# Two row tiles of each of the first two experts closed with the sixth chunk of tokens

## The chip, the cores and the metric

The kernel runs on one core of a Trainium2 chip. The metric is the device time of one execution in microseconds (us), as a median of runs. The engines are TensorE (PE in the profile; its weight loads are PEld), VectorE (DVE), ScalarE (ACT), GpSimd (POOL) and SyncE (SP), which issues most of the DMA transfers.

## What is computed

Three layers follow one another on 2304 tokens: attention over 32 memory slots (`q`, `k`, `v`, `phi`; 4 batches of 576 tokens), a gated layer of width 1536 (`moe_w_gate`, `moe_w_val`, `moe_w_out`), and a mixture of eight experts with two experts chosen for each token. The change touches the last layer alone. Its input `x` is the output of the gated layer, 2304 x 512:

```python
logits = x @ w_gate
noise_scale = np.log1p(np.exp(x @ w_noise))
noisy_logits = logits + noise_scale * noise
top2 = np.argpartition(-noisy_logits, 2, axis=1)[:, :2]
...
for e in range(E):                       # E = 8 experts, F = 1024
    for k in range(2):
        mask = top2[:, k] == e
        h = np.maximum(x[mask] @ w1[e], 0.0)
        out[mask] += top2_w[mask, k, None] * (h @ w2[e])
```

## The kernel before

**Tokens.** The gated layer is done in two stages. `stage1` (line 412) makes the gated activations `gT`, `stage2` (435) multiplies them by `w_out` for one tile of 128 tokens at a time (18 tiles), into a PSUM tile `px`. Two tiles are a chunk, nine chunks in all (0 to 8). When a tile's `px` is complete, `tokens` (446) scales it and splits it into two float16 halves (`row`, on ScalarE and VectorE), writes it to the table `xs` in HBM, and has it transposed by a DMA into `xt`; then TensorE computes its router logits (`pl`, twelve small products, line 472), and once a chunk's two tiles are there `route` (526) finds the two best experts of each token. It counts the rows of each expert with small products on TensorE (`pk`, lines 570 to 573, which need the VectorE tile `o` of line 565), and GpSimd scatters each token's number and weight into the table `meta` at the slot that the count gives (four indirect DMAs per chunk, line 588).

**Experts.** Each expert has 624 slots, as five row tiles of 128, 128, 128, 128 and 112. For a row tile the kernel reads its token numbers from `meta` (`fetch`, 735, tile `mts`), gathers the rows from `xs` by GpSimd (`gather`, 749, tile `xg`, four buffers), and has SyncE transpose them (`turn`, 756) into the columns of `xe`, which has two buffers, one per expert. `first2` (759) multiplies `xe` by `w1` in eight steps `f`, each of 12 matmuls per span of columns, and ScalarE and VectorE turn the result `ph` into the hidden tile `hT` (770 to 772). `second2` (774) multiplies `hT` by `w2`, 24 matmuls of 512 columns per row tile, into `py`; ScalarE scales it into `y` (785) and GpSimd adds it to the output in HBM by a scatter (786). `moe2` (809) runs over the eight experts.

**Rows before the last token.** So that TensorE has work while the last tokens are routed, a part of the rows is closed early: after chunk `SNAP` the count of an expert is raised, if it is lower, to the number of early slots (lines 595 to 603), so that those slots are settled. Before, three tiles of expert 0 (`EARLY = 3`) are closed with the seventh chunk (`SNAP = 6`): `early_rows` (794) gathers and transposes them, the first product of 384 columns runs in `build` (1055), then the late rows are fetched, and the second products of the three tiles run (1066) while expert 0's last two tiles are gathered. `moe2` then does the other 240 columns of expert 0, its two last tiles, and the other experts with two spans of 312 columns.

**Weights.** Experts 0 and 1 have their weights split into float16 halves beforehand; they are loaded by line 733 into `w1a`, `w2a`, `w1b`, `w2b`. From expert 2 on `splits` (683) does it beside the products: each quarter of a weight is loaded into one of seven buffers (`wo`, line 675), squared and summed (701, 703), the sum goes through a small product on TensorE (`pmx`, line 86), and the quarter is split into `w1a`, `w2a`, `w1b` or `w2b` (378, 379) when the expert that used that buffer is through.

**Order.** Each engine runs its queue in order. A scheduler places the instructions by the order and the priorities of the program; the `yield`s of `tokens` and `route` (`WAIT_TURN`, `WAIT_ROUTE`, and their shorter `..._LAST` forms from chunk `SNAP` on) say how many steps later TensorE's part follows.

Of the kernel before, what the change touches and what calls it, by code (L numbers as in the profile page):

```python
# [10 lines left out]
F32 = mybir.dt.float32  # L11
# [5 lines left out]
ALU = mybir.AluOpType  # L17
# [8 lines left out]
E, F2 = 8, 1024  # L26
P = 128
# [3 lines left out]
F2T = F2 // P  # L31
CH = 256
# [7 lines left out]
ST = 5  # L40

TAIL = 112
SLOT = (ST - 1) * P + TAIL
PADS = ST * P

EARLY = 3
SNAP = 6

AHEAD2 = 2

# [15 lines left out]
class Kern:  # L66
# [379 lines left out]
    def tokens(self, c, t):  # L446
# [18 lines left out]
        nc.sync.dma_start_transpose(xt, row.rearrange("p a b -> p (a b)"))  # L465
        for _ in range(WAIT_TURN if c < SNAP else WAIT_TURN_LAST):
            yield
# [58 lines left out]
    def route(self, c, lg, it):  # L526
        nc, rp = self.nc, self.rp
# [27 lines left out]
        mt = rp.tile([P, nt, 2, 2], I32, tag="mt", name="mt")  # L555
# [9 lines left out]
        nc.vector.tensor_tensor(o, oh[:, :, 0, :], oh[:, :, 1, :], op=ALU.add)  # L565
        for _ in range(WAIT_ROUTE if c < SNAP else WAIT_ROUTE_LAST):
            yield
        pk = self.pr.tile([P, 512], F32, tag="pr", name="pk")[:, : nt * E].rearrange("p (t e) -> p t e", t=nt)
# [17 lines left out]
        for t in range(nt):  # L586
            for k in range(2):
# [6 lines left out]
                self.scatters.append(d)  # L594
        if c == SNAP:

            pk = self.pr.tile([P, 512], F32, tag="pr", name="pk")
            nc.tensor.matmul(pk[:1, :1], self.ones[:, :1], self.oacc[:, :1], start=True, stop=True)
            fr = rp.tile([1, 1], F32, tag="fr", name="fr")
            nc.vector.tensor_scalar(fr, pk[:1, :1], -1.0, float(EARLY * P), op0=ALU.mult, op1=ALU.add)  # L600
            nc.vector.tensor_scalar(fr, fr, 0.0, None, op0=ALU.max)
            nc.vector.tensor_tensor(self.oacc[:1, :1], self.oacc[:1, :1], fr, op=ALU.add)
            self.snapped = True


# [186 lines left out]
        others.append(d)  # L792

    def early_rows(self):
        xg = [self.gather(self.mt[(0, i)], PADS + (SNAP + 1) * CH) for i in range(EARLY)]
        yield
        yield
        for i in range(EARLY):
            yield
            self.turn(xg[i], self.xe[0], i)  # L800

    def xe_tile(self, e):
        self.xe[e] = self.mx.tile([P, 2 * KT, ST * P], F16, tag="xe", name="xe")
# [5 lines left out]
    def moe2(self):  # L809

        self.freed, self.nparts = [0, 0], 0
        self.splitter = self.splits()
        mt, xe, xg = self.mt, self.xe, {}
        for e in range(E):
            nx = e + 1
            if nx < E:
                self.xe_tile(nx)
                if e:
                    self.fetch(nx, 0, ST, self.scatters)
                for i in range(4):  # L820
                    xg[i] = self.gather(mt[(nx, i)])
            spans = [(0, SLOT // 2), (SLOT // 2, SLOT)] if e else [(EARLY * P, SLOT)]
            for f in range(F2T):
                self.first2(self.w1[e % 2], xe[e], f, spans)
                self.step2(2)
            self.freed[0] = e + 1
            todo = list(range(0 if e else EARLY, ST))
            sums = [] if e else self.sums0
            turns = list(range(ST)) if nx < E else []
            for n, i in enumerate(todo):  # L830
                self.second2(self.w2[e % 2], self.iw[:, e : e + 1], mt[(e, i)], i, sums, P if i < ST - 1 else TAIL)
                for _ in range(-(-len(turns) // (len(todo) - n))):
                    j = turns.pop(0)
                    self.turn(xg[j], xe[nx], j)
                    if j == 0:
                        xg[4] = self.gather(mt[(nx, 4)])
                self.step2(3)
            self.freed[1] = e + 1
# [61 lines left out]
    def build(self):  # L900
        tc, nc, ctx = self.tc, self.nc, self.ctx
# [27 lines left out]
        side, offset = [], {}  # L929

        def ahead_by(n):
            return tc.high_priority(n) if n else ExitStack()

        def step(n=1):
            for _ in range(n):
                for g in list(side):
                    with ahead_by(offset.get(g, 0)):
                        done = next(g, self) is self
                    if done:
                        side.remove(g)  # L940
# [40 lines left out]
        def first(b, u, ch):  # L981
            while self.tokens_ready < b * S + (ch + 1) * QC:
                turns(atts)
            if (b, u) not in self.wq:
                self.fold(b, u)
            self.stage1(b, u, ch)
# [19 lines left out]
        def beside():  # L1006
            nonlocal pre
            step()
            turns(atts)
            if pre is None and self.attended == B:  # L1010
                for _ in atts:
                    pass
                self.att_ctx.close()
                self.presplit_open()
                pre = start(self.presplits())
            if self.snapped and not self.mt:
                self.fetch(0, 0, EARLY, self.scatters)
                rows.append(start(self.early_rows()))

        def second(*Ts):  # L1020
            for T in Ts:
                for fs in (range(0, 4), range(4, 8), range(8, 12)):
                    self.stage2(T, list(fs))
                    beside()
                g = start(self.tokens(*divmod(T, CH // P)))
                if T >= NT - CH // P:
                    offset[g] = AHEAD

        for b in range(1, B):
            second(*range(3 * (b - 1) // 2 * TB, 3 * b // 2 * TB))  # L1030
            if b == B - 1:
                while pre is None:
                    beside()
                drain(pre)
                self.ps_ctx.close()
                self.early_open()
                self.wload2(0, 0)
                for e in range(AHEAD2):
                    self.inverse_scale(e)
                self.xe_tile(0)  # L1040
            self.fold(b, 0)
            for u in range(UN):
                if u + 1 < UN:
                    self.fold(b, u + 1)
                for ch in range(S // QC):
                    first(b, u, ch)
                    beside()
            self.folded = b + 1
# [3 lines left out]
        second(*range(3 * (B - 1) // 2 * TB, NT))  # L1052
        while not rows or rows[0] in side:
            beside()
        for f in range(F2T):
            self.first2(self.w1[0], self.xe[0], f, [(0, EARLY * P)])
            beside()
        while side:
            step()
        self.fetch(0, EARLY, ST, self.scatters)  # L1060
        late = [self.gather(self.mt[(0, i)]) for i in range(EARLY, ST)]
        self.wload2(1, 0)
        self.wload2(1, 1)
        self.fetch(1, 0, ST, self.scatters)
        self.sums0 = []
        for i in range(EARLY):
            self.second2(self.w2[0], self.iw[:, 0:1], self.mt[(0, i)], i, self.sums0)
            if i >= EARLY - len(late):
                j = i + len(late)
                self.turn(late[j - EARLY], self.xe[0], j)  # L1070
        self.moe2()
        self.overflow()
        self.ring_ctx.close()
# [30 lines left out]
```

## Time and profile before

| | us |
|---|---|
| Median of three runs (905.08 to 908.67) | 905.18 |
| The profiled execution's own time | 898.48 |
| Its span, first to last instruction | 896.7 |
| PE busy in the span | 813.6 (91%) |
| VectorE, ScalarE, GpSimd busy | 470.7, 450.4, 207.5 |

TensorE is busy for nine tenths of the span, so the time is its work and its gaps. A row of a timeline gives the start, the length, the engine, the line, what is written from what, and in brackets how long the engine sat idle before it and what ended that. In the view by stretches PEclk is the share of full speed that TensorE's clock was granted: 1.00 is 2.4 GHz, 0.50 is 1.2 GHz. Times are us from the start of the span.

### The profile page before, as it was taken

Reading aid. Unit: us, or ns where it says so; the run is one execution under the profiler, and the core shown is the slowest. Engines: PE = TensorE matmul, PEld = TensorE weight load, DVE = VectorE, ACT = ScalarE, POOL = GpSimd, SP = SyncE. Lnnn points to the kernel's source line nnn. Section 1 sums busy time; section 2 is a strip of 40 time slices with the busy share of each in tenths; the row PEclk is TensorE's granted clock in tenths of the full one; section 3 lists DMA queues with packets and bytes.
Section 4 is the critical chain, followed back from the end, with each engine's and each line's share of the span. In section 5 each row is a group of like instructions: output and inputs, shape, how many; then the busy total and the mean of one; then the engine's idle time right before and its main releaser. Section 6 shows DMA issues by size and latency. Waiting matters only on the chain. (4 is left out here: it accounts for less than half of the span.)

```text
span 896.7 us, 16818 instructions
## 1 busy us (share of the span) xinstructions
PE 813.6 (91%) x6531; PEld 534.5 (60%) x6531; DVE 470.7 (52%) x1317; ACT 450.4 (50%) x909; POOL 207.5 (23%) x210
## 2 busy tenths in 40 slices
PE   5368789889999999999959999999999999999995
PEld 4247665579645775687425666564746556574752
DVE  1778786576446986875433245463544346340110
ACT  3578675455333873763114456464545446461320
POOL 1544440020002120120132530232323122232112
PEclk9998789999999999999979999999999999999998
DMA  9598739710263566605782993686566867473213
GB/s 310 161 287 255 220 122 353 208 54 2 68 195 75 190 205 172 212 2 154 223 201 59 208 226 106 140 190 162 116 181 132 167 140 205 78 112 49 27 14 45
DMA packets 125922, 135.15 MB, mean 151 GB/s; under 512 B 71824, under 2 KB 88336, under 8 KB 125328
## 3 DMA queue, kind: packets, MB, share of 16 engines
q1 hardware_dynamic: 115856, 113.30, 44.4%
q0 software_dynamic: 9984, 20.75, 13.1%
q8 instruction: 52, 0.85, 0.4%
q14 instruction: 30, 0.25, 0.1%
HBM read 87.97 MB, written 30.86 MB: 133 GB/s over the span
## 5 line engine op out<-in xcount | busy, mean ns | idle before, releaser
L426 PE MATMUL pg<-x,wq 128*128 128x192 f16 x1728 | 168.5, 258 | 25.4 <-DVE wq L379 7.3
L426 PEld LDWEIGHTS <-wq 128*128 128x128 f16 x1728 | 151.8, 103 | 43.9 <-ACT wq L378 21.0
L780 PEld LDWEIGHTS <-hT 128*128 128x128 f16 (+1 forms) x960 | 100.0, 105 | 106.0 <-DVE hT L772 1.5
L444 PE MATMUL px<-wo,gT 128*128 128x512 f16 x648 | 147.3, 379 | 1.5 <-DVE wo L379 0.8
L786 POOL DMA_INDIRECT out<-y,mts x40 | 63.5, 1587 | 228.8 <-ACT y L785 227.6
L766 PE MATMUL ph<-xe,w1a 128*128 128x312 f16 (+2 forms) x768 | 105.4, 299 | 10.0 <-DMA xe<-xg 10.0
L772 DVE TENSOR_TENSOR hT<-r,hT 128x312 f16<-128x312 f32 (+2 forms) x128 | 56.6, 479 | 93.9 <-ACT hT L771 93.4
L780 PE MATMUL py<-w2a,hT 128*128 128x512 f16 (+1 forms) x480 | 104.9, 379 | 1.0 <-DVE hT L772 1.0
L780 PE MATMUL py<-w2b,hT 128*128 128x512 f16 (+1 forms) x480 | 104.7, 379 | 0.0
L444 PEld LDWEIGHTS <-gT 128*128 128x128 f16 x648 | 62.1, 98 | 71.1 <-issue 3.9
L766 PE MATMUL ph<-xe,w1b 128*128 128x312 f16 x768 | 103.0, 296 | 0.1
L766 PEld LDWEIGHTS <-w1a 128*128 128x128 f16 x768 | 75.5, 99 | 38.5 <-issue 10.5
L770 ACT ACTIVATE r<-ph 128x312 f32<-128x312 f32 (+2 forms) x128 | 49.0, 429 | 87.5 <-PE ph L766 78.8
L785 ACT ACTIVATE y<-py,css 128x512 f32<-128x512 f32 (+1 forms) x40 | 27.5, 687 | 128.5 <-PE py L780 124.0
L766 PEld LDWEIGHTS <-w1b 128*128 128x128 f16 x768 | 75.2, 98 | 27.0 <-issue 0.3
L588 POOL DMA_INDIRECT meta<-mt,vi x36 | 36.7, 1019 | 186.8 <-DVE vi L585 114.6
L751 POOL DMA_INDIRECT xg<-xs,mts x40 | 45.7, 1142 | 70.7 <-DMA xe<-xg 26.2
L783 DVE TENSOR_TENSOR css<-mts,iw 128x1 f32<-128x1 f32 (+1 forms) x40 | 6.6, 167 | 90.6 <-ACT y L785 88.6
L771 ACT CAST hT<-r 128x312 f16<-128x312 f32 (+2 forms) x128 | 52.4, 460 | 0.4
L432 ACT ACTIVATE gT<-pg 128x384 f16<-128x384 f32 x72 | 35.0, 486 | 34.0 <-DVE pg L431 34.0
L433 DVE SCALAR_TENSOR_TENSOR gT<-pg,gT 128x384 f16<-128x384 f32 x72 | 39.8, 553 | 18.4 <-ACT gT L432 17.7
L378 ACT ACTIVATE wq<-pv,ws 128x256 f16<-128x256 f32 x96 | 42.1, 471 | 11.3 <-DVE wq L379 6.5
(311 smaller groups left out, 961.3 us busy)
## 6 DMA issues: line engine op xcount, KB each, us to landing
wo<-w SPq DMA_DIRECT2D x48, 512.0 KB, 5.5
st<-kv SPq DMA_DIRECT2D x16, 512.0 KB, 6.0
f<-w SPq DMA_DIRECT2D x16, 512.0 KB, 5.8
wsp<-hl SPq DMA_DIRECT2D x16, 512.0 KB, 3.5
w<-wg SPq DMA_DIRECT2D x12, 512.0 KB, 5.7
w<-wv SPq DMA_DIRECT2D x12, 512.0 KB, 5.8
w<-wo SPq DMA_DIRECT2D x12, 512.0 KB, 4.6
out<-z SPq DMA_DIRECT2D x23, 256.0 KB, 5.2
```

Of the source, the lines that this page charges most:

```text
L378: self.nc.scalar.activation(hi, src, AF.Copy, scale=sc)
L426: nc.tensor.matmul(p[:, f, :], w[:, l, g, j, f * P : (f + 1) * P], x[:, r, g, ch * QC : (ch + 1) * QC], start=n == 0, stop=n == 5)
L433: nc.vector.scalar_tensor_tensor(o[:, 1, :, cols], pv, 2.0 ** -16, o[:, 0, :, cols], op0=ALU.mult, op1=ALU.subtract)
L444: nc.tensor.matmul(p, g[:, l, f % 2, t * P : (t + 1) * P], self.wob[f // 2][:, r, f % 2, :], start=f + i == 0, stop=f == FT - 1 and i == 2)
L588: d = nc.gpsimd.indirect_dma_start(out=self.meta, out_offset=bass.IndirectOffsetOnAxis(ap=vi[:, t, k : k + 1], axis=0), in_=mt[:, t, k, :] ...
L751: self.nc.gpsimd.indirect_dma_start(out=xg.rearrange("p a b -> p (a b)"), out_offset=None, in_=self.xs[:rows, :], in_offset=bass.IndirectO ...
L766: nc.tensor.matmul(p[:, : t1 - t0], w1[:, l, k, f * P : (f + 1) * P], xe[:, x, t0:t1], start=n == 0, stop=n == 3 * KT - 1)
L770: nc.scalar.activation(r, p[:, : t1 - t0], AF.Relu, scale=2.0 ** -19)
L771: nc.scalar.copy(self.hT[:, 0, f, t0:t1], r)
L772: nc.vector.tensor_sub(self.hT[:, 1, f, t0:t1], r, self.hT[:, 0, f, t0:t1])
L780: nc.tensor.matmul(py, self.hT[:, l, f, i * P : i * P + m], w2[:, w, f, :], start=n == 0, stop=n == 3 * F2T - 1)
L786: d = nc.gpsimd.indirect_dma_start(out=self.out, out_offset=bass.IndirectOffsetOnAxis(ap=mt[:m, 0:1], axis=0), in_=y[:m], in_offset=None, ...
```

## The change

The constants become two early tiles of two experts, closed with the sixth chunk. `route` raises the counts of both experts (`EX` columns in place of one), `early_rows` gathers and transposes four tiles, and `beside` fetches the numbers of both. In `build` the early part of expert 0 and of expert 1 run one after the other, first and second product each; between the two the late rows of both experts are fetched, and expert 0's are gathered and transposed. `moe2` starts with the other three tiles (368 columns) of expert 0, and then those of expert 1, in one span each. The number of matmuls is the same (96 per span in place of 96 and 96 for expert 0 and of 192 for expert 1).

```diff
-EARLY = 3
-SNAP = 6
+EARLY, EX = 2, 2
+SNAP = 5
...
-            nc.tensor.matmul(pk[:1, :1], self.ones[:, :1], self.oacc[:, :1], start=True, stop=True)
+            nc.tensor.matmul(pk[:1, :EX], self.ones[:, :1], self.oacc[:, :EX], start=True, stop=True)
...
-        xg = [self.gather(self.mt[(0, i)], PADS + (SNAP + 1) * CH) for i in range(EARLY)]
+        tiles = [(e, i) for e in range(EX) for i in range(EARLY)]
+        xg = [self.gather(self.mt[t], PADS + (SNAP + 1) * CH) for t in tiles]
...
         for e in range(E):
-            nx = e + 1
-            if nx < E:
+            nx, old = e + 1, EARLY if e < EX else 0
+            turns = list(range(EARLY if nx < EX else 0, ST)) if nx < E else []
+            if nx >= EX and nx < E:
                 self.xe_tile(nx)
-                if e:
-                    self.fetch(nx, 0, ST, self.scatters)
-                for i in range(4):
-                    xg[i] = self.gather(mt[(nx, i)])
-            spans = [(0, SLOT // 2), (SLOT // 2, SLOT)] if e else [(EARLY * P, SLOT)]
+                self.fetch(nx, 0, ST, self.scatters)
+            for i in turns[:4]:
+                xg[i] = self.gather(mt[(nx, i)])
+            spans = [(0, SLOT // 2), (SLOT // 2, SLOT)] if not old else [(old * P, SLOT)]
...
-        for f in range(F2T):
-            self.first2(self.w1[0], self.xe[0], f, [(0, EARLY * P)])
-            beside()
-        while side:
-            step()
-        self.fetch(0, EARLY, ST, self.scatters)
-        late = [self.gather(self.mt[(0, i)]) for i in range(EARLY, ST)]
         self.wload2(1, 0)
         self.wload2(1, 1)
-        self.fetch(1, 0, ST, self.scatters)
-        self.sums0 = []
-        for i in range(EARLY):
-            self.second2(self.w2[0], self.iw[:, 0:1], self.mt[(0, i)], i, self.sums0)
-            if i >= EARLY - len(late):
-                j = i + len(late)
-                self.turn(late[j - EARLY], self.xe[0], j)
+        self.sums = [[] for _ in range(E)]
+        self.xg = {}
+        for e in range(EX):
+            for f in range(F2T):
+                self.first2(self.w1[e], self.xe[e], f, [(0, EARLY * P)])
+                beside()
+            for i in range(EARLY):
+                self.second2(self.w2[e], self.iw[:, e : e + 1], self.mt[(e, i)], i, self.sums[e])
+                beside()
+            if e == 0:
+                while side:
+                    step()
+                for x in range(EX):
+                    self.fetch(x, EARLY, ST, self.scatters)
+                for i in range(EARLY, ST):
+                    self.xg[i] = self.gather(self.mt[(0, i)])
+                for i in range(EARLY, ST):
+                    self.turn(self.xg[i], self.xe[0], i)
         self.moe2()
```

How this moves the queues. On TensorE, before, the 384 columns of expert 0 stand in runs of 29, 32 and 35 matmuls around the last tokens' `pl` and the last chunk's `pk`; now runs of 12, 51 and 33 matmuls of 256 columns stand there, the last `pk` comes five matmuls into expert 0's second product, and the rest of that (43), expert 1's first (96) and second product (48) stand before the late 368 columns.

SyncE's queue after the weights `w1a` are loaded, in the time of the sixth chunk, before (`xs` and `xt` belong to a token tile):

```order
L733 DMA w1a<-wsp 128x8192
L733 DMA w2a<-wsp 128x8192
L462 DMA xs<-row 128x1024
L465 DMA_TRANSPOSE xt<-row 128x8x128
L733 DMA w1b<-wsp 128x8192
```

and now:

```order
L733 DMA w1a<-wsp 128x8192
L739 DMA mts<-meta 128x4 x2
L757 DMA_TRANSPOSE xe<-xg 128x8x128 x4
L733 DMA w2a<-wsp 128x8192
L462 DMA xs<-row 128x1024
```

The early rows' two fetches and four transposes have come to stand ahead of the load of `w2a` and of the seventh chunk's tokens.

SyncE's queue at the last two token tiles, before (`wo` are the quarters of expert 2's weights):

```order
L739 DMA mts<-meta 128x6
L675 DMA wo_71<-w 128x1024
L462 DMA xs<-row 128x1024
L465 DMA_TRANSPOSE xt<-row 128x8x128
L675 DMA wo_72<-w 128x1024
L757 DMA_TRANSPOSE xe<-xg 128x8x128 x3
L675 DMA wo_73<-w 128x1024
L675 DMA wo_74<-w 128x1024
L462 DMA xs<-row 128x1024
L465 DMA_TRANSPOSE xt<-row 128x8x128
```

and now:

```order
L675 DMA wo_71<-w 128x1024
L462 DMA xs<-row 128x1024
L465 DMA_TRANSPOSE xt<-row 128x8x128
L675 DMA wo_72<-w 128x1024
L675 DMA wo_73<-w 128x1024
L675 DMA wo_74<-w 128x1024
L675 DMA wo_75<-w 128x2x512
L675 DMA wo_76<-w 128x2x512
L462 DMA xs<-row 128x1024
L465 DMA_TRANSPOSE xt<-row 128x8x128
L739 DMA mts<-meta 128x6 x2
```

The early fetch and the three early transposes are gone from between the two tiles, and all five loads that were left stand ahead of the last tile.

GpSimd's queue from the last two chunks' scatters on, before (`out<-y` is a row tile's scatter into the output):

```order
L588 DMA meta<-mt,vi 18560x2 x8
L751 DMA xg<-xs,mts 128x1024 x4
L786 DMA out<-y,mts 2944x512
L751 DMA xg<-xs,mts 128x1024 x4
L786 DMA out<-y,mts 2944x512
```

and now:

```order
L588 DMA meta<-mt,vi 18560x2 x8
L786 DMA out<-y,mts 2944x512
L751 DMA xg<-xs,mts 128x1024 x4
L786 DMA out<-y,mts 2944x512
L751 DMA xg<-xs,mts 128x1024 x6
```

The first scatter of an early tile has moved ahead of the gathers of the late rows.

## Rows read from the trace of the kernel before

**Rows 1.** By stretch: us; busy PE, PEld, DVE, ACT, POOL; PEclk; DMA share; GB/s
```profile
456.07:575.96 119.89, 107.01 (x666) 64.71 (x666) 49.27 (x147) 54.85 (x107) 36.25 (x33) 0.96 0.72 166
...
466.00:471.00 5.00, 3.96 (x13) 1.90 (x14) 0.00 (x0) 0.00 (x0) 0.97 (x1) 0.50 1.09 286
...
500.00:505.00 5.00, 3.14 (x22) 1.95 (x21) 0.16 (x1) 0.69 (x1) 1.67 (x2) 1.00 1.16 219
```

**Rows 2.** PE in order of time: start us, us, what [idle before <-releaser]
```profile
457.35 0.17 PE L570 MATMUL pk<-o,tri 128*128 128x8 f16 x1 [1.28 <-DVE o L565]
...
458.32 0.46 PE L472 MATMUL pl<-wr,xt 128*128 128x16 f16 x12 [0.80 <-DMA xt<-row]
...
467.04 6.98 PE L766 MATMUL ph<-xe,w1a 128*128 128x384 f16 x29 [8.17 <-DMA xe<-xg]
...
474.16 5.36 PE L766 MATMUL ph<-xe,w1a 128*128 128x384 f16 x32
...
480.19 0.18 PE L570 MATMUL pk<-o,tri 128*128 128x8 f16 x1 [0.67 <-DVE o L565]
...
486.01 15.70 PE L780 MATMUL py<-w2a,hT 128*128 128x512 f16 x72
...
503.58 10.01 PE L766 MATMUL ph<-xe,w1a 128*128 128x240 f16 x96 [1.86 <-DMA xe<-xg]
...
575.80 9.70 PE L766 MATMUL ph<-xe,w1a 128*128 128x312 f16 x72
```

**Rows 3.** The chain that ended last, at the late rows: start us, us, what
```profile
487.10 0.97 POOL meta L588
...
491.94 4.72 DMA xg<-xs,mts
...
496.67 1.23 SPq L757
...
498.01 5.52 DMA xe<-xg
```

**Rows 4.** SyncE's queue in order of time, around the last tokens
```profile
414.42 0.33 SPq L733 DMA_DIRECT2D w2a<-wsp  x1
...
460.29 4.00 SPq L757 DMA_TRANSPOSE xe<-xg  x3
...
466.14 2.18 SPq L465 DMA_TRANSPOSE xt<-row  x1
```

**Rows 5.** The nine transposed token tiles (xt), time from issue to landing
```profile
DMA to landing us min/median/max: 4.2/4.6/6.5
```

**Rows 6.** VectorE in order of time, in the routing of the last two chunks
```profile
452.75 0.23 DVE L783 TENSOR_TENSOR css<-mts,iw 128x1 f32<-128x1 f32 x2 [1.96 <-DMA mts<-meta]
...
458.00 0.68 DVE L456 TENSOR_REDUCE am<-px 128x1 f32<-128x512 f32 x1
...
460.53 0.75 DVE L461 SCALAR_TENSOR_TENSOR row<-px,tts,row 128x512 f16<-128x512 f32 x1
...
479.96 0.17 DVE L565 TENSOR_TENSOR o<-oh 128x16 f16<-128x16 f32 x1
```

**Rows 7.** The sixth chunk: PE's wait, its prefix products, GpSimd's last scatter
```profile
382.24 4.23 PE L426 MATMUL pg<-x,wq 128*128 128x192 f16 x48 [1.34 <-ACT sg L429]
...
389.42 0.17 PE L570 MATMUL pk<-o,tri 128*128 128x8 f16 x1
...
397.58 0.96 POOL L588 DMA_INDIRECT meta<-mt,vi  x1 [0.32 <-issue]
```

**Rows 8.** Expert 2's weights: VectorE in order of time, then one piece of the chain
```profile
525.75 3.68 DVE L379 SCALAR_TENSOR_TENSOR w1a<-wo,sc2s,w1a 128x1024 f16<-128x1024 f32 x3 [0.88 <-ACT w1a L378]
...
534.44 1.23 DVE L701 SCALAR_TENSOR_TENSOR w2a<-wo 128x1024 bf16<-128x1024 f32 x1 [2.95 <-DMA wo<-w]
...
536.38 0.15 DVE L706 TENSOR_REDUCE sm<-sq 128x1 f32<-128x4 f32 x1
...
529.33 5.09 DMA wo<-w
```

More of the change, by code (lines that the diff above doesn't have):

```diff
@@ L597, in route @@
             pk = self.pr.tile([P, 512], F32, tag="pr", name="pk")
-            nc.tensor.matmul(pk[:1, :1], self.ones[:, :1], self.oacc[:, :1], start=True, stop=True)
-            fr = rp.tile([1, 1], F32, tag="fr", name="fr")
-            nc.vector.tensor_scalar(fr, pk[:1, :1], -1.0, float(EARLY * P), op0=ALU.mult, op1=ALU.add)
+            nc.tensor.matmul(pk[:1, :EX], self.ones[:, :1], self.oacc[:, :EX], start=True, stop=True)
+            fr = rp.tile([1, EX], F32, tag="fr", name="fr")
+            nc.vector.tensor_scalar(fr, pk[:1, :EX], -1.0, float(EARLY * P), op0=ALU.mult, op1=ALU.add)
             nc.vector.tensor_scalar(fr, fr, 0.0, None, op0=ALU.max)
-            nc.vector.tensor_tensor(self.oacc[:1, :1], self.oacc[:1, :1], fr, op=ALU.add)
+            nc.vector.tensor_tensor(self.oacc[:1, :EX], self.oacc[:1, :EX], fr, op=ALU.add)
             self.snapped = True
@@ L794, in early_rows @@
     def early_rows(self):
-        xg = [self.gather(self.mt[(0, i)], PADS + (SNAP + 1) * CH) for i in range(EARLY)]
+        tiles = [(e, i) for e in range(EX) for i in range(EARLY)]
+        xg = [self.gather(self.mt[t], PADS + (SNAP + 1) * CH) for t in tiles]
         yield
         yield
-        for i in range(EARLY):
+        for x, (e, i) in zip(xg, tiles):
             yield
-            self.turn(xg[i], self.xe[0], i)
+            self.turn(x, self.xe[e], i)
     def xe_tile(self, e):
@@ L826, in moe2 @@
             self.freed[0] = e + 1
-            todo = list(range(0 if e else EARLY, ST))
-            sums = [] if e else self.sums0
-            turns = list(range(ST)) if nx < E else []
+            todo = list(range(old, ST))
             for n, i in enumerate(todo):
-                self.second2(self.w2[e % 2], self.iw[:, e : e + 1], mt[(e, i)], i, sums, P if i < ST - 1 else TAIL)
+                self.second2(self.w2[e % 2], self.iw[:, e : e + 1], mt[(e, i)], i, self.sums[e], P if i < ST - 1 else TAIL)
                 for _ in range(-(-len(turns) // (len(todo) - n))):
@@ L1016, in beside @@
             if self.snapped and not self.mt:
-                self.fetch(0, 0, EARLY, self.scatters)
+                for e in range(EX):
+                    self.fetch(e, 0, EARLY, self.scatters)
                 rows.append(start(self.early_rows()))
@@ L1039, in build @@
                     self.inverse_scale(e)
-                self.xe_tile(0)
+                for e in range(EX):
+                    self.xe_tile(e)
             self.fold(b, 0)
@@ L1054, in build @@
             beside()
-        for f in range(F2T):
-            self.first2(self.w1[0], self.xe[0], f, [(0, EARLY * P)])
-            beside()
-        while side:
-            step()
-        self.fetch(0, EARLY, ST, self.scatters)
-        late = [self.gather(self.mt[(0, i)]) for i in range(EARLY, ST)]
         self.wload2(1, 0)
         self.wload2(1, 1)
-        self.fetch(1, 0, ST, self.scatters)
-        self.sums0 = []
-        for i in range(EARLY):
-            self.second2(self.w2[0], self.iw[:, 0:1], self.mt[(0, i)], i, self.sums0)
-            if i >= EARLY - len(late):
-                j = i + len(late)
-                self.turn(late[j - EARLY], self.xe[0], j)
+        self.sums = [[] for _ in range(E)]
+        self.xg = {}
+        for e in range(EX):
+            for f in range(F2T):
[13 more added lines that the diff above has]
+                    self.turn(self.xg[i], self.xe[0], i)
         self.moe2()
```

## The prediction

> **What bounds the kernel now.** I read the shares of busy time first, then TensorE's waits in order of time, then the chain that ended last. TensorE (PE) is the bound nearly everywhere, so a change that leaves its matmuls alone can give back only idle time and slow clock. The stretch that the change rewrites runs from the end of the last token tile's product (456.07, which is 457.35 less the 1.28 of idle in front of it [rows 2]) to expert 2's first product at 575.8 [rows 2]: 119.89 us, of which PE is busy 107.01, so 12.88 are idle [rows 1]. Five waits make up 12.8 of them: 1.28 on VectorE's `o` for the last but one chunk's `pk`, 0.80 for a transposed token tile, 8.17 for expert 0's early rows, 0.67 on `o` of the last chunk, 1.86 for expert 0's late rows [rows 2]. The 8.17 cost more than themselves: over 466 to 471 the granted clock is 0.50, that is 1.2 GHz [rows 1], and the 29 matmuls of 384 columns behind the wait take 6.98 us, where 32 of them take 5.36 a little later [rows 2]. At 5.36/32 = 0.1675 the 29 are 4.9, so the clock costs 2.1. Idle and clock together: 15.0 us. The chain that ended last goes through the late rows: last scatter, fetch, gather, transpose, and at the end of it the product at 503.58 [rows 2, 3].
>
> **The products themselves: nothing.** Per matmul: 0.1675 us at 384 columns, 10.01/96 = 0.104 at 240, 9.70/72 = 0.135 at 312, 15.70/72 = 0.218 at 512 [rows 2]. Between the first two a column is worth 0.00044, so 256 columns are 0.111 and 368 are 0.160. Before: 96 x 0.1675 + 96 x 0.104 + 192 x 0.135 = 52.0. After: 192 x 0.111 + 192 x 0.160 = 52.0. The second products are the same ten row tiles.
>
> **Early rows, sixth chunk.** Their fetches and transposes now stand in SyncE's queue ahead of the load of `w2a`, which left at 414.42 [rows 4], and of all later tokens. Who waits behind them: that load and the seventh chunk's tokens. Latest bound: even if the sixth chunk's scatters came no earlier than before (the last at 397.58 [rows 7]), the first gather is 4.8 behind (487.10 to 491.94 [rows 3]), three more at about the 1.3 that a transpose takes (4.00 for three [rows 4]), 4.7 for the rows and 1.3 for the last transpose: 412.5, before 414.42. In fact PE's order has the chunk's `pl` and `pk` (389.42 [rows 7]) some hundred matmuls earlier, so they come sooner still. Whether the 1.34 of PE waiting on ScalarE there [rows 7] goes, or comes a second time because the routing's small steps now fall between other evacuations, the rows do not say: -1.3 to +1.3, taken as 0. So the 8.17 and its 2.1 of clock go: the rows are there some 45 us early. What is late next are the router's products.
>
> **The last token tile.** PE's work behind 456.07 is now 63 matmuls of 256 columns with `pl` and `pk` between them, 7.0 + 0.5: it reaches the last tile's `pl` at about 463.6. VectorE began on that tile at 458.00, because 1.96 us before it had stood for the numbers of the early rows (452.75); its part was done at 460.53 + 0.75 = 461.28, 3.3 later [rows 6]. The wait for these numbers is gone from there, so I take the start as 456.2 and the end as 459.5. SyncE then was busy with the three early transposes at 460.29 and sent the tile's own at 466.14 [rows 4]; now only weight loads stand before it, and it goes at about 459.9. Landing takes 4.2 to 6.5 [rows 5], with these loads in flight more likely above the median of 4.6: I take 5.5, 465.4, a wait of 1.8. Bounds: 464.1, no wait worth naming, to 461.7 + 6.5 = 468.2, a wait of 4.6. This takes the place of the waits of 1.28 and 0.80, since 12 of the 63 matmuls stand before that `pk`.
>
> **The last `pk`.** From the end of `pl` (474.3, just ahead of the run at 474.16 [rows 2], whose head overlaps it) to `o` (479.96 + 0.17 [rows 6]) were 5.8 us. PE now has 33 x 0.111 + 5 x 0.218 = 4.8 between, so it waits about 1.2 (0.67 as before to 2.0, since more steps of VectorE's `hT` stand between).
>
> **The late rows.** From that `pk` (480.19 [rows 2]) to the late rows' arrival (498.01 + 5.52 [rows 3]) were 23.4 us; expert 0 now needs a third tile, one transpose more, 24.7. Behind `pk` PE has 43 x 0.218 + 96 x 0.111 + 48 x 0.218 = 30.5 us of early work. So 5.8 are to spare and the 1.86 goes. GpSimd now has the first early scatter in front of the gathers, which waits for `y`; that tile's last matmul comes 19 x 0.218 = 4.1 behind `pk`, the gathers were 11.8 behind it (480.19 to 491.94 [rows 2, 3]), so this costs nothing while it stays under 11.
>
> **Expert 2's weights.** Expert 0's late product ends at X (513.6 before, 503.58 + 10.01 [rows 2]); only then do `w1a` and `xe`'s first buffer come free. SyncE first has to send expert 2's five transposes; the next weight quarter behind them went at about 529.3 and took 5.09, VectorE stood 2.95 for it, and the sum that it completes was ready at 536.38 + 0.15, X + 22.9 [rows 8]. PE needs that sum for a `pmx` that now stands behind 72 x 0.218 + 36 x 0.160 = X + 21.5. If nothing of this gets faster PE waits 1.5 us; but the quarter's buffer is freed by the split at 525.75 [rows 8], whose own `pmx` comes two row tiles behind X as before, while four of the five gathers are now long done. I take 0.3, bounds 0 and 1.5.
>
> **Sum.** 15.0 gone, 1.8 + 1.2 + 0.3 = 3.3 new: 11.7 us saved. The profiled execution, 898.48, becomes 886.8. The median of the runs is 905.18, 6.7 above it for reasons that one profile cannot show; I take the same saving from it: **893.5**. Best: the early stretch gives 1.3 and only the 0.67 stays, 15.6, 889.6. Worst, with every upper bound and 2.1 of clock for the longer wait: 15.0 - 4.6 - 2.1 - 2.0 - 1.5 - 1.3 = 3.5, 901.7.
>
> **Rivals.**
> 1. *The wait moves to the last token tile.* `xt` lands as late as the worst row (4.6 of idle) and the clock falls with it (2.1); with 1.2 and 0.3 that is 8.2, a saving of 6.8: 898.4, and 901.7 with all bounds. For it: five weight loads go just ahead of the tile. Against it: the three gathers that shared the DMA engines with it before are gone. 15%.
> 2. *The late rows are not covered.* The four `xg` buffers and the scatters in GpSimd's queue stretch 24.7 beyond 30.5; each further us is one of idle. At twice the spare, 36.3, it takes 5.8: 899.3. Against it: the first round of gathers finds all four buffers empty. 6%.
> 3. *The clock stays down, slower than before.* The place is the run behind the wait at 464: if the clock falls there and the groups of 12 matmuls, each into another PSUM bank, do not bring it back until the late rows, 33 x 0.111 + 91 x 0.218 + 96 x 0.111 = 34 us of work take 34 more: 927. It decides against the change once 11.7 us of full-clock work run at half. Against it: behind the 1.86 wait the clock is 1.00 over 500 to 505 [rows 1], the 96 narrow matmuls there, in the same groups, run at 0.104, and the run at 474.16 is at full rate though the one before it began at 0.50 [rows 1, 2]. 4%. By the Trainium skill, page "TensorE: Matmul & The Clock Gate", section "A second HAM failure mode: psum-queue depth-cycling", a kernel that goes from bank to bank idles for moments between its groups and the clock swings down and up; that would be this rival. The traced product of 240 columns does not show it.
> 4. *The rows are not there.* If fewer than 256 rows of an expert came in the first six chunks, padding would fill the early slots, and an expert could run over its 624. Counted from the reference's own routing, the first 1536 tokens give experts 0 and 1 384 and 341 rows, and all tokens 589 and 527. Below 1%.
>
> **How the numbers follow.** The forecast has 74%. 0.5% is 4.5 us, about what a measurement of this kernel can tell from no change, so faster means below 900.65. There lie the forecast, two thirds of rival 1 and half of rival 2: 0.87. Same is the rest of these two: 0.08. Slower is rival 3 and what I have not named: 0.05. The range 889.5 to 900.5 reaches from the best sum to most of rivals 1 and 2, and leaves out their tails and rival 3.
>
> **What would show it.** In the profile of the changed kernel: no PE wait on `xe` at all, or one under 1 us; clock 1.00 from the last token tile on; one wait of 0 to 4 us for `xt` near 464 and one near 1 us on `o`; four early transposes on SyncE before `w2a` leaves; expert 2's first product about 11.7 earlier, near 564; the stretch from there to the end as long as before. It is wrong if a wait on `xe` over 3 us remains, if PE waits over 2 us at the `pmx` in expert 1's late product, or if the time behind expert 2's start grows.

## The result and the profile after

The changed kernel takes 895.34 us (median of 4 runs, 893.75 to 899.66) against 905.13 of before: a ratio of 0.9892 with a 95% interval of 0.9848 to 0.9936. The forecast was 893.5, the range 889.5 to 900.5, so the time came out as predicted. The profiled execution is another matter: 893.75 us (span 891.9) stands against 898.48 (span 896.7) of before, a saving of 4.7 where the sum said 11.7. Expert 2's first product comes at 571.28, 4.5 earlier than before, and not the 11.7 (near 564) that the prediction named as its sign.

The stretch that the prediction is about, by stretches of after (us; busy PE, PEld, DVE, ACT, POOL; PEclk; DMA share; GB/s), as [rows 1]:

```profile
462.24:571.28 109.04, 106.01 (x665) 64.59 (x664) 45.49 (x129) 53.91 (x103) 38.84 (x33) 0.98 0.74 165
...
472.00:477.00 5.00, 4.74 (x40) 3.73 (x41) 1.25 (x7) 2.31 (x6) 0.83 (x1) 0.66 0.01 0
500.00:505.00 5.00, 5.00 (x25) 2.26 (x24) 0.85 (x2) 1.51 (x4) 2.89 (x3) 1.00 1.10 238
```

The last token product now ends at 462.24, where the early products begin, and expert 2 begins at 571.28: 109.04 us with 3.0 of idle, where [rows 1] has 119.89 with 12.88. TensorE in order of time in that stretch of after, as [rows 2]:

```profile
462.24 1.47 PE L766 MATMUL ph<-xe,w1a 128*128 128x256 f16 x12
...
463.98 5.73 PE L766 MATMUL ph<-xe,w1a 128*128 128x256 f16 x51
472.26 0.49 PE L472 MATMUL pl<-wr,xt 128*128 128x16 f16 x12 [2.54 <-DMA xt<-row]
472.60 5.17 PE L766 MATMUL ph<-xe,w1a 128*128 128x256 f16 x33
...
479.06 0.18 PE L570 MATMUL pk<-o,tri 128*128 128x8 f16 x1 [0.21 <-DVE o L565]
...
509.31 15.12 PE L766 MATMUL ph<-xe,w1a 128*128 128x368 f16 x96
...
546.02 0.35 PE L86 MATMUL pmx<-sm,onef 128*128 128x1 f32 x2 [0.27 <-DVE css L783]
...
571.28 4.01 PE L766 MATMUL ph<-xe,w1a 128*128 128x312 f16 x29
```

No wait for `xe` is left: neither for the early rows at 462.24 nor for the late ones at 509.31. Three small waits stand in for the five of [rows 2]: 2.54 for `xt`, 0.21 on `o`, 0.27 at a `pmx`. So the late part did what was forecast. But its beginning, 462.24, is 6.2 us *later* than the 456.07 of before, and the loss lies ahead of it, in the last 18 of the 72 gate steps (`stage1`; counted here from 0, so steps 54 to 71). There ScalarE shows two waits of a kind that the first trace of before has not. ScalarE, then GpSimd, in order of time in after (start us, us, what, idle before and releaser; "remote" is a releaser that the profile cannot name):

```profile
379.61 0.84 ACT L378 ACTIVATE wq<-pv,ws 128x256 f16<-128x256 f32 x2 [3.48 <-remote]
...
391.73 0.84 ACT L378 ACTIVATE wq<-pv,ws 128x256 f16<-128x256 f32 x2 [3.51 <-remote]
```

```profile
377.67 0.96 POOL L588 DMA_INDIRECT meta<-mt,vi  x1 [0.30 <-issue]
...
389.66 0.97 POOL L588 DMA_INDIRECT meta<-mt,vi  x1 [0.30 <-issue]
```

Each wait ends about 1 us behind the last of four scatters that GpSimd issues back to back: 379.61 - 378.63 = 1.0 and 391.73 - 390.63 = 1.1. ScalarE needs nothing from GpSimd there. It waits for a small product of TensorE, `pv`, which by its own record ended at 375.84:

```profile
374.77 1.07 PE L240 MATMUL pv<-w,vb 64*32 64x256 f32 x22 [0.16 <-DVE spl L539]
```

I call such a wait a hold. TensorE, which bounds the kernel, pays for the first one behind it, since its next gate step needs the tanh that ScalarE could not yet make:

```profile
381.72 1.31 PE L426 MATMUL pg<-x,wq 128*128 128x192 f16 x14 [3.50 <-ACT sg L429]
```

From the tanh of step 54 to that of step 71 TensorE is idle 7.2 us, against 1.5 in the first trace of before. The experiments had to say whether the holds belong to the change, to that execution, or to the indirect DMAs.

### The profile page after: what moved, and what is told of

Read it like the earlier page. It is cut to its first block, busy times and chain, and to the rows that moved or that the text cites. A ratio compares the mean times of both kernels' runs of the same rounds, so it can differ in the third digit from the quotient of the medians.

```text
span 891.9 us, 16833 instructions
## 1 busy us (share of the span) xinstructions
PE 813.2 (91%) x6531; PEld 532.9 (60%) x6531; DVE 472.2 (53%) x1317; ACT 451.0 (51%) x909; POOL 208.9 (23%) x210
## 5 line engine op out<-in xcount | busy, mean ns | idle before, releaser
L426 PEld LDWEIGHTS <-wq 128*128 128x128 f16 x1728 | 149.7, 102 | 48.9 <-ACT wq L378 20.7
L766 PE MATMUL ph<-xe,w1b 128*128 128x312 f16 (+2 forms) x768 | 103.0, 296 | 0.0
L751 POOL DMA_INDIRECT xg<-xs,mts x40 | 45.3, 1132 | 87.9 <-DMA xe<-xg 53.1
```

Of the source, the lines that this page charges most:

```text
L426: nc.tensor.matmul(p[:, f, :], w[:, l, g, j, f * P : (f + 1) * P], x[:, r, g, ch * QC : (ch + 1) * QC], start=n == 0, stop=n == 5)
L751: self.nc.gpsimd.indirect_dma_start(out=xg.rearrange("p a b -> p (a b)"), out_offset=None, in_=self.xs[:rows, :], in_offset=bass.IndirectO ...
L766: nc.tensor.matmul(p[:, : t1 - t0], w1[:, l, k, f * P : (f + 1) * P], xe[:, x, t0:t1], start=n == 0, stop=n == 3 * KT - 1)
```

## The experiments

All traces are compared by three points that each has: the start of ScalarE's tanh of gate step 54, that of step 71, and the Relu behind expert 2's first product. Worked out from the 14 traces:

| Kernel (name of its expectation) | steps 54 to 71, us | step 71 to expert 2, us | median, us (runs) | ratio to before in the same session (95%) |
|---|---|---|---|---|
| before, first trace | 41.1 | 165.5 | 905.1 (4) | |
| before, second trace (before_again) | 47.7 | 164.6 | 904.0 (12) | 1.0029 (0.9998 to 1.0060) |
| changed, first trace | 50.7 | 154.5 | 895.3 (4) | 0.9892 (0.9848 to 0.9936) |
| changed, second trace (again) | 48.4 | 154.9 | 893.4 (6) | 0.9891 (0.9839 to 0.9943) |
| old_waits | 48.2 | 155.2 | 892.4 (6) | 0.9889 (0.9846 to 0.9932) |
| chunk7 | 45.3 | 166.8 | 902.4 (10) | 1.0000 (0.9968 to 1.0032) |
| snap_only | 49.8 | 157.4 | 899.6 (10) | 0.9957 (0.9917 to 0.9997) |
| late_gather | 51.0 | 154.6 | 894.1 (12) | 0.9925 (0.9894 to 0.9956) |
| late_rows | 51.0 | 155.6 | 897.5 (12) | 0.9948 (0.9925 to 0.9971) |
| twice | 62.5 | 154.3 | 906.1 (10) | 1.0047 (1.0015 to 1.0079) |
| rows_held | 46.1 | 166.8 | 899.5 (12) | 0.9953 (0.9912 to 0.9993) |
| rows_held2 | 42.6 | 167.4 | 899.3 (12) | 0.9976 (0.9941 to 1.0010) |
| before_held2 | 40.9 | 164.6 | 896.7 (12) | 0.9925 (0.9885 to 0.9964) |
| rows_order | 43.0 | 158.5 | 891.8 (12) | 0.9935 (0.9904 to 0.9965) |

From expert 2 to the end all of them take 316 to 318 us. The first 54 gate steps and all before them, code that none of the edits touches, put step 54 anywhere from 365.7 to 379.7 us: one trace's total says little, a stretch of it says more.

**Once more, unchanged.**

> The changed kernel once more, nothing edited. Its trace starts 3.1 us ahead of before's at the tanh steps of the last batch's second stage (about 369 us) and is 6.5 us behind nine such steps later (about 403 us): 9.6 us lost in a stretch that the prediction took as 0 with 1.3 either way. Theory A, the code: the sixth chunk's router steps stand earlier there (the short waits of the last chunks now hold from the sixth chunk on), and the same 9 to 10 us are lost again at the same steps; time 894 to 897. Theory B, that one execution: the two stalls of 3.5 us of ScalarE, both while four scatters of GpSimd run, don't come back; the loss is 0 to 4 us, and the time 886 to 891.

The second trace loses time at the same steps: one hold of 3.39 us ends 1.0 behind the fourth scatter.

```profile
393.47 0.84 ACT L378 ACTIVATE wq<-pv,ws 128x256 f16<-128x256 f32 x2 [3.39 <-remote]
```

The stretch takes 48.4, still 7.3 over the first trace of before. Not an accident of one execution of the changed kernel, then, though the time, 893.4, fits neither theory's range: it lies 0.6 under that of theory A.

**The old order of the sixth chunk's steps.**

```
-        for _ in range(WAIT_TURN if c < SNAP else WAIT_TURN_LAST):
+        for _ in range(WAIT_TURN if c < 6 else WAIT_TURN_LAST):
...
-        for _ in range(WAIT_ROUTE if c < SNAP else WAIT_ROUTE_LAST):
+        for _ in range(WAIT_ROUTE if c < 6 else WAIT_ROUTE_LAST):
```

> The changed kernel with one thing undone: the short waits of the token and router steps hold from the seventh chunk on, as before the change, so the sixth chunk's steps stand among the gate steps where they stood before. The snapshot is still the sixth chunk's. Theory A (the early steps cost the 9.6 us): the stretch takes as long as in before, within 2 us, and the time is 886 to 889 (895.3 less 7 to 9). Theory B (that one execution): 894 to 897 in the median, as the changed kernel, with the stretch within 2 us of the repeat's. The snapshot comes one unit later, which costs nothing in either unless the gathered rows miss the early products at 457 us.

48.2 us and, within the noise, the same time as the repeat (892.4 against 893.4): the order of the router's steps is not the cause, and theory A falls.

**The snapshot back at the seventh chunk.**

```
-SNAP = 5
+SNAP = 6
```

> The changed kernel with the snapshot back at the seventh chunk; two row tiles of each of two experts, and both experts' products between the last tokens and the late rows, stay. By the theory of the prediction the 8 us wait for the early transposes comes back in full (their chain starts with the same scatters as in before, and has four tiles in place of three: 8.2 to 9.5), while the other gaps stay covered by expert 1's early products, and the gate stretch is as before: 905 less 12.9 and 2.1, plus 3 of new waits, plus 8 to 10, is 901 to 903. Rival: products are covered by nothing else that moves, and the wait is hidden since something else is late: under 897.

As expected: 902.4, with the wait for the early rows back in full.

```profile
473.69 8.31 PE L766 MATMUL ph<-xe,w1a 128*128 128x256 f16 x56 [7.90 <-DMA xe<-xg]
```

Unasked, it told more. Its gate steps are those of before in the same order, and yet they take 45.3 against 41.1, with a hold behind the sixth chunk's scatters.

**The sixth chunk alone.**

```
 EARLY = 3
-SNAP = 6
+SNAP = 5
```

> The kernel before with one thing alone: the three early row tiles of the first expert are closed with the sixth chunk in place of the seventh. The 8.2 us wait for the early transposes goes; the gaps at the late rows (1.3, 0.8, 0.7, 1.9 us) stay. By theory A the gate stretch also loses 9 to 10 us: 905 to 907. By theory B it loses 0 to 4: 897 to 901.

The wait of 8.17 is gone and the late stretch takes 157.4, 8.1 less than in the first trace of before and 7.2 less than in the second; the late rows are awaited as they were:

```profile
497.69 2.53 PE L766 MATMUL ph<-xe,w1a 128*128 128x240 f16 x23 [2.52 <-DMA xe<-xg]
```

So by this stretch the two parts of the change are worth 7.2 to 8.1 (the chunk) and a further 2.5 to 2.9 (expert 1's products as cover: 154.5 and 154.9); the cover without the chunk is worth nothing (chunk7, 166.8). The medians of one session put 6.2 between this kernel and the changed one, where both stretches together give 3.9; that difference is not explained. The median, 899.6, lies in theory B's range and under theory A's, while the gate steps, 49.8, show the loss that B denied. The ranges had been reckoned from a before at 905, and before took 901.9 beside these runs, so the median decides little between them.

**A second trace of before.**

> The kernel before, nothing edited, for a second trace of it. From the tanh of step 56 to that of step 64 of the gate steps (374.07 to 396.38 in the first trace, 22.3 us) theory C (any indirect DMA that GpSimd issues there holds up the other engines, and the first trace escaped) expects 25 to 28 us, with waits of ScalarE of 2 to 4 us that end about 1 us behind the fourth scatter, as in the trace with the snapshot at the seventh chunk, which has the same steps there (26.5 us). Theory A (only the moved steps cost it) expects 22.3 within 1 us. Its time is 898 to 905 either way.

It came out in the main as theory C says: steps 55 to 63 (56 to 64 in the expectation, which counts from 1) take 27.3 us where the first trace has 22.3, and ScalarE is held with GpSimd's scatters. The longer of the two waits shown ends before the fourth of them, which runs from 399.78 to 400.75; the short one ends 1.1 behind it:

```profile
399.54 0.47 ACT L378 ACTIVATE wq<-pv,ws 128x256 f16<-128x256 f32 x1 [2.34 <-PE pg L426]
...
401.86 0.58 ACT L429 ACTIVATE sg<-pg,gs 128x384 f32<-128x384 f32 x1 [0.75 <-remote]
```

```profile
399.78 0.97 POOL L588 DMA_INDIRECT meta<-mt,vi  x1 [0.30 <-issue]
```

The exception was the first trace of before. Steps 54 to 71 differ by 6.66 us between the two; its profiled execution lay 6.65 under the median of its runs. That the two figures meet is no proof: the profiled execution of before_held2 below lies 7.7 under its median too, and its gate steps have nothing to lose.

**Later gathers, later scatters (written later only).**

```
-            if self.snapped and not self.mt:
+            if self.snapped and not self.mt and self.folded == B:
```

> The changed kernel with the four gathers of the early rows, and the loads and transposes with them, held back until the last batch's gate steps are over (about 420 us in place of 394). Scatters stay where they are. Theory C: the part of the loss at the gathers goes, 1.2 to 2.6 us, and the time is 890.5 to 892 (the repeat measured 893.4). Theory A: nothing changes in the gate steps, 893 to 894. If the transposes then come behind the last rows of tokens on SyncE's queue, a wait for them at about 457 us gives 1 to 4 us back.

> The changed kernel with the sixth chunk's four scatters held back too until the gate steps are over, and the gathers behind them. Theory C: the stall of 3.4 us that ends 1 us behind those scatters goes with that of the gathers: 5 to 6 us less than the repeat, 887 to 889, and ScalarE has no wait over 2 us behind 385 us in the gate steps. Theory A: as the repeat, 893 to 894. Against both: SyncE's queue then waits for scatters and gathers where the last rows of tokens want it, and a wait at 430 to 457 us takes back 1 to 5 us.

The second kernel has also `while c == SNAP and self.folded < B: yield` ahead of the scatter loop. Neither tested what it was made for: nothing in the data keeps these DMAs back, and the scheduler put them where they had stood (gathers from 394.39 and 395.43, the sixth chunk's scatters from 384.40 and 385.38 us). Hence gate steps of 51.0 in both. Where nothing moves, both theories give the repeat's time, and 894.1 for the first agrees with that; that the second is 3.4 slower is not explained.

**The sixth chunk's scatters twice.** Behind the loop of scatters, for the sixth chunk only:

```
+                    d = nc.gpsimd.indirect_dma_start(
+                        out=self.meta2, out_offset=bass.IndirectOffsetOnAxis(ap=vi[:, t, k : k + 1], axis=0),
+                        in_=mt[:, t, k, :], in_offset=None)
```

> The changed kernel with the sixth chunk's four scatters issued a second time, into a table that nothing reads (the indices and rows are the same, no engine waits for the four new ones). They take GpSimd 5.1 us more in the gate steps. Theory C: a second hold of 2 to 5 us, 895.5 to 898.5. Theory A, and any theory by which GpSimd's issue is hidden behind the others' work: 893 to 894.

Far worse than theory C had it (895.5 to 898.5): 906.1, which is 12.0 more than late_gather and 8.6 more than late_rows, the two kernels of the same session with gate steps of 51.0. In the trace the gate steps take 62.5, 11.5 more, and the granted clock over them is 0.84 (0.97 in the first trace of the changed kernel), so a part of the loss is slow clock behind the hold. The four extra scatters close the gap between scatters and gathers, so twelve indirect DMAs run back to back from 396.71 to 411.62, and ScalarE stands until 2.6 us behind them. ScalarE, then TensorE and GpSimd towards the end of it:

```profile
414.21 0.84 ACT L378 ACTIVATE wq<-pv,ws 128x256 f16<-128x256 f32 x2 [12.02 <-remote]
```

```profile
408.92 0.48 PE L426 MATMUL pg<-x,wq 128*128 128x192 f16 x2 [1.09 <-issue]
...
409.65 0.32 PE L426 MATMUL pg<-x,wq 128*128 128x192 f16 x1 [0.26 <-issue]
...
410.67 0.95 POOL L762 DMA_INDIRECT xg<-xs,mts  x1 [0.30 <-issue]
411.05 0.48 PE L426 MATMUL pg<-x,wq 128*128 128x192 f16 x2 [1.08 <-issue]
...
411.77 0.32 PE L426 MATMUL pg<-x,wq 128*128 128x192 f16 x1 [0.25 <-issue]
414.12 0.64 PE L426 MATMUL pg<-x,wq 128*128 128x192 f16 x3 [2.04 <-issue]
```

TensorE too gets one or two matmuls done at a time, with waits that the profile can pin on nothing ("issue"), while GpSimd issues. (This execution, 915.5, was the slowest of the ten and lay 9 us over their median; most of that is ahead of step 54, which it reached at 379.7. The price of 8.6 to 12.0 rests on the medians, not on it.)

**Scatters that really wait.** The tanh is kept as `self.last`, and the scatters of the fifth and sixth chunks get a dependence on the last of them, in the changed kernel (rows_held: the sixth chunk only) and in before. The two changed kernels keep the later fetch of late_gather as well; before has no other edit:

```
+        while 4 <= c <= 5 and self.folded < B:
+            yield
...
+                if 4 <= c <= 5:
+                    self.follow(d, [self.last])
```

> The changed kernel with the sixth chunk's four scatters made to wait for the tanh of the last gate step, so that they, and the loads, gathers and transposes behind them, really run after the gate steps (written later alone, in the kernel with late rows, the scheduler had put them back at 385 to 400 us). Theory C (indirect DMAs of GpSimd hold the other engines up in the gate steps): from the tanh of step 54 to that of step 71 it takes 43 to 45 us in place of 48.4 and 50.7 in the two traces of the changed kernel, and the time is 887 to 889 against its 893.4 to 895.3. Against it: the hold only moves to the tokens behind and costs the same there, 893 to 895; or the transposes land late and TensorE waits for them before the early products, with 1 to 5 us given back.

> As the kernel with the sixth chunk's scatters behind the last gate step, and the fifth chunk's four scatters there too: no indirect DMA is left from step 54 to step 71. Theory C: that stretch takes 41 to 43 us (41.1 in the first trace of before, which showed no hold), and the time is 884 to 887. Any theory by which the order of the router's steps alone is the cost: the stretch stays at 48 to 51 us, and the time at 893 to 895. The chain to the early transposes is 5 us longer than with four scatters, so a wait of 0 to 4 us before the early products can come in place of the holds.

> The kernel before with the scatters of the fifth and sixth chunks made to wait for the tanh of the last gate step, nothing else: its early rows hang on the seventh chunk's scatters, which stay where they are. Theory C: the stretch from step 54 to 71 takes 41 to 42 us in place of the 47.7 of the second trace of before, and the time is 895 to 898 against 904.0. With the two kernels that hold scatters it gives what the late rows' cover is worth when the gate steps are undisturbed: 10 to 12 us between this one and the changed kernel without holds. Rival: 903 to 905, and the stretch as in the second trace.

This shows that the indirect DMAs among the gate steps are the cause of the loss there. With none of them among the gate steps these take 40.9 us in the kernel before and 42.6 in the changed one; with the fifth chunk's left in, 46.1. Before gains 7.5 us by it, 896.7 against 904.2 of before in the same session. The changed kernel loses by it: 899.5 and 899.3 miss the 887 to 889 and 884 to 887 of theory C by 10 us and more, and the ratios to before, 0.9953 and 0.9976, are worse than its 0.9892. The rival named there came, and larger than the 1 to 5 us it was given: SyncE now stands until 423.77 for the row numbers and from 427 to 435 for the gathers, and the rows of tokens queue behind. SyncE, then TensorE, of rows_held2:

```profile
423.77 0.81 SPq L743 DMA_DIRECT2D mts<-meta  x2
424.63 0.43 SPq L462 DMA_DIRECT2D xs<-row  x1
...
435.15 4.00 SPq L761 DMA_TRANSPOSE xe<-xg  x3
439.25 0.53 SPq L462 DMA_DIRECT2D xs<-row  x1
```

```profile
428.26 0.49 PE L472 MATMUL pl<-wr,xt 128*128 128x16 f16 x12 [4.19 <-DMA xt<-row]
...
443.23 0.47 PE L472 MATMUL pl<-wr,xt 128*128 128x16 f16 x12 [3.34 <-DMA xt<-row]
```

What the gate steps give, 5.8 to 8.1 us against the two traces of the changed kernel, the late stretch takes back and more: 167.4 against 154.7.

**The queue put in order.** The loads of row numbers are set behind the second token tile's transpose, those of the early rows behind the third's, by dependences that only order the queue:

```
+            self.behind(d, 13)
...
+        while 14 not in self.xts:
+            yield
         for x, (e, i) in zip(xg, tiles):
+            self.behind(self.turn(x, self.xe[e], i), 14)
```

> The kernel with the scatters of the fifth and sixth chunks behind the last gate step, and SyncE's queue put in an order that doesn't make rows of tokens wait for them: the loads of the early row numbers stand behind the transposed row of the second token tile after the gate steps, the four early transposes behind that of the third. Theory C, with the queue as the only reason why holding the scatters had not paid: gate steps of 41 to 43 us from step 54 to 71, no wait for a transposed token row over 1 us before the early products and up to 3 for the last tile's, early products 44 to 46 us behind the last gate step; 886 to 889 us, faster than both kernels. If something else made the held kernels slow (the 2 MB loads beside the gathers, late gathers): 893 to 899, with waits for transposed rows of tokens or of the experts between 425 and 460 us.

43.0 us for the gate steps, and most of the late stretch is back, 158.5. Of the rest, most is one wait: the four transposes took 9.65 us of SyncE's queue (6.85 in the first trace of the changed kernel), and the fourth token tile came behind them. SyncE, then TensorE:

```profile
442.81 9.65 SPq L763 DMA_TRANSPOSE xe<-xg  x4
452.56 0.53 SPq L462 DMA_DIRECT2D xs<-row  x1
```

```profile
448.58 0.49 PE L472 MATMUL pl<-wr,xt 128*128 128x16 f16 x12 [3.44 <-DMA xt<-row]
```

891.8 misses the 886 to 889 expected. It is the lowest median here, but before was faster in that session too (897.6), and the ratio of 0.9935 is no better than 0.9892. It isn't shown to beat the changed kernel. Nor is its trace a test of the holds, since it shows none anywhere (see the last section); before_held2 and rows_held2 are that test.

## Why the prediction was right

By its own steps:

- **15.0 of idle and slow clock gone:** right. None of the five waits of [rows 2] is left in its old place and size. The sum of this part, 11.7, compares with 119.89 less 109.04 = 10.9 in the traces.
- **The last token tile, 1.8 of wait:** right, 2.54 (2.38 in the repeat). SyncE sent the tile at 465.62 where the estimate, moved by the 6.2 of later start, says 466.1. A small piece of rivals 1 and 3 came with it, which the sum had at nothing: behind this wait the granted clock is 0.66 over 472 to 477 and 33 matmuls take 5.17 us. In the repeat the clock is 1.00 there and 33 take 3.76, so 1.4 us went that way, and not in every execution. The clock is 1.00 again over 500 to 505, and before that over 490 to 499, in the products of 256 columns, so rival 3 itself did not come. The Trainium skill, page "TensorE: Matmul & The Clock Gate", section "A second HAM failure mode: psum-queue depth-cycling", warns of a clock that swings in a kernel that goes from bank to bank; this stretch does not show it.
- **The last `pk`, 1.2, and expert 2's weights, 0.3:** 0.21 and 0.27. The 0.21 lies under its lower bound of 0.67 (in the repeat it is 1.73, inside 0.67 to 2.0); the 0.27 is right.
- **The late rows, covered:** right, no wait at 509.31. Rivals 2 and 4 did not come, and rival 1 only in the small piece above.
- **Early rows, sixth chunk, taken as 0 with 1.3 either way:** this step failed. Against the profile that the sum was made on, the gate steps lost 9.6 us (50.7 against 41.1) and 7.3 in the repeat. The reason given there, small steps of routing between other evacuations, was sound for these steps: with no indirect DMA among them, steps 55 to 63 take 22.37 us in rows_held2 and 22.31 in the first trace of before. What failed is the price of the DMAs: they were costed as places in a queue and as landings. That GpSimd's indirect DMAs hold engines that do not wait for GpSimd was in no term, and [rows 7] showed the scatters of the one execution that escaped.
- **The same saving from the median:** this is why the total held. The median of before was 6.7 over its profile "for reasons that one profile cannot show". The second trace shows one of that size: 6.66 us of holds in the gate steps. By the 12 runs of before_held2, which are 7.5 us shorter without them, before pays them in most runs; that they are the 6.7 of that first session is likely, not shown. Against it the changed kernel's loss is not 9.6 but 0.7 to 3.0 (48.4 and 50.7 against 47.7), and 10 of late saving less that leaves 7 to 9, where the medians show 9.8 and, in the repeat's session, 8.4. Had the sum been held to its own base, 886.8 from 898.48, it would have been 7 us off.

So the forecast was right in the mechanism of the late stretch, and its size in the median was right partly by luck: two things left out of it, the holds in before and in the changed kernel, nearly cancel.

## What to carry to other kernels

Before a profile becomes the base of a sum, ask why it differs from the median of the runs: 6.7 us, over half of the saving in question, is about what one stretch differed by between two executions of the same kernel. Indirect DMAs that GpSimd issues have a price beyond their own rows when they fall among short steps that hand results from TensorE to ScalarE to VectorE; behind a long run of independent matmuls the same scatters were nearly free (before_held2). And to move a transfer in scheduled code it takes a dependence, not a later line, and then the queue it waits in must be looked at, or the gain comes back as waits of whatever stands behind it.

## What the runs showed of the hardware

In the traces with holds, four scatters back to back (4.8 us of GpSimd, 0.97 each) hold ScalarE's next use of a product by 2.3 to 3.5 us, in the changed kernel until some 1.0 us behind the last of them; twelve back to back held it 12.0 us, until 2.6 behind, and TensorE's own matmuls came singly meanwhile. The Trainium skill, page "Trainium Architecture — The Big Picture", section "What this means for kernel authors", says that the engines are independent processors, and that a matmul on TensorE does not block a copy on VectorE unless a semaphore stands between them. For GpSimd's indirect DMAs the traces with holds disagree: no instruction of ScalarE or TensorE waits there for those scatters, and yet both stand for 3 us and more. The Trainium skill, page "Perfetto Trace Analysis", section "Tensor Engine Instruction (MATMUL, LD_WEIGHTS)", says that a matmul's recorded end is computed from its size, and that the semaphore goes out only when the results are acknowledged. The trace agrees with that gap: `pv` is recorded as done at 375.84 and ScalarE went on at 379.61.

The traces also list when each semaphore, the counter through which an engine tells others that a result is there, was counted up. In the first trace of the changed kernel TensorE's counts for the two halves of `pv`, recorded as done at 375.46 and 375.84, come at 379.59 and 379.63, and the count for a group of `pg` that is recorded as done at 377.24 comes at 379.76. Twelve matmuls, 1.0 us of work, lie between the last two of these, and their counts are 0.13 apart: the work had been done, and word of it was late. In none of the 14 traces is a count of VectorE, ScalarE or GpSimd more than 0.03 us behind the recorded end. So a hold there is TensorE's count that comes late, which ScalarE and then TensorE itself wait for.

The same list parts the traces into two kinds. In 12 of them TensorE's counts come late (0.5 to 4.1 us, 13.5 in twice) beside indirect DMAs all through the kernel, already near 190 us in code that no edit touches; and of the counts that the four engines should show, 60 to 86 are missing from the record, every one of them during an indirect DMA or within 2.5 us behind one. In the other two, the first trace of before and that of rows_order, no count of TensorE is more than 0.46 late and at most two are missing. So the first trace of before did not escape at one spot, where its scatters stand against the same products at the same spacing as in the second (393.75 to 398.54, `pv` at 393.73): that whole execution has no holds.

What makes an execution one or the other kind is open. So is whether the recording of the counts has a part in the holds, as records that are lost at the same places suggest: no run here is known to have gone without it, and the medians, 7.5 us less without the scatters and 8.6 to 12.0 more with four added, show the cost only for executions as they were measured. Nor do these runs separate GpSimd's issue of an indirect DMA from the transfer that it starts.
